# Spectral layer and squared-ReLU FFN: rows turned by DMA transposes in two chunks, preparation by numbered slots, and a drain in halves of columns

## The chip, the cores and the metric

One core of a Trainium2 chip. Times are device microseconds of a launch, medians of several runs on one chip; the profile's span is about 1.7 us shorter. Every run told of here is of the fast state. The granted TensorE clock was 0.995 to 1.000 in all of them but three, which had 0.99: two of the last experiment (e11) and one of the kernel before; they are named where they count. Everywhere else the clock plays no part.

## The reference

x has 2048 rows of 512, weights and results are bf16. B_x is not used.

```python
h  = x + irfft2(rfft2(layernorm(x)) * (w_r + 1j * w_i))
u  = layernorm(h)
h2 = h + square(relu(u @ w1 + b1)) @ w2 + b2          # w1: 512 x 1792, w2: 1792 x 512
```

## The kernel before

The transforms are matmuls in six steps. Steps 1 to 4 fill T2 (the change touches only one filler matmul there; a filler is a matmul without use, put into a gap). The rows are then taken in 16 groups of 128. For each group: `s5` (TensorE) and a copy to V and H (ScalarE), `s5b` makes R of it (VectorE), `s6` multiplies R by KI (TensorE), `s6a` adds x (VectorE), `s6b` takes statistics, `norm` makes u. u is turned (128 x 128 blocks transposed) into UT, which the FFN needs as its moving operand. TensorE writes into PSUM, from where the other engines copy. GpSimd makes hb = h + b2, which VectorE adds to the FFN's result.

The FFN goes in five chunks of 2, 3, 4, 4 and 3 groups. A chunk has 14 "up" pieces (4 matmuls each) and then its "downs" (14 matmuls a group). While one chunk is computed, the next one is prepared in between. In the traces here an engine's pieces follow in the order of the program (in e6 below a turn placed one slot later also runs after the last down), so where a piece stands in the program decides what waits for it.

```python
def transp(c, half):                      # TensorE turns, ScalarE and VectorE copy out of PSUM
    pt = bank("p7", "pp", 3, BF16)
    for d in range(2):
        for i in range(n):
            o = P * (n * d + i)
            nc.tensor.transpose(pt[:, o:o + P], us[c][:, i, bass.ts(2 * half + d, P)], ident[:])
    ...                                   # half 0: nc.scalar.copy, half 1: nc.vector.tensor_copy

def up(f):
    ph = bank("ph", "ph", 3)
    ...                                   # 4 matmuls W1 x UT -> ph
    nc.scalar.activation(rl[:, 0:n], ph[:, 0:n], ACT.Relu, bias=b1f[:, f:f + 1], scale=1.0)
    sq = nc.vector.tensor_tensor(act[:, f, 0:n], rl[:, 0:n], rl[:, 0:n], ALU.mult)
    mine = [a + f // 3] if c and f % 3 == 1 and f // 3 < b - a else ...
    for g in mine:                        # GpSimd, not before this square
        add = nc.gpsimd.tensor_tensor(hb[:, g, :], hs[:, g, :], b2b[:], ALU.add)

PLAN = {1: ((-3.33, 'ahead', 0), (-0.19, 's5b', 1), ...),  # estimated us; for chunk 1 from the start of chunk 0, for the others from the end of the chunk before
        ...}

# the drain: groups 0 and 1 alone, after the last of step 4
s5_first(0); s5_whole(1); s5b(0); s6(0); s6(1)
rest = [s5(2, True), s5(3, True)]
s6a(1); s6b(0, True); s6b(1)
...                                       # fillers, roots, norms, 8 transposes, 2 copies
for c in range(5):
    run(c)
```

## Time and profile before

| | before |
|---|---|
| time, median of 7 | 166.53 us |
| span | 164.8 us |
| first FFN matmul starts | 53.65 us |
| last FFN matmul ends | 161.49 us |
| end of the last addition on VectorE to the end of the span | 2.80 us |

Two things to read first: where TensorE, busy 93% of the span, has gaps (they can be closed), and what it does in the stretches without gaps (that can only be taken away). The prediction below shows the lines. Start of the first up of a chunk to start of the next one's is a ruler used throughout; it is 14.48, 22.01, 26.83 and 26.16 us for chunks 0 to 3.

### The profile page before, as it was taken

The page shows a single profiled execution, that of the slowest core. Times are in us where ns is not written, and L with a number is a line of the kernel's source. Part 1 is how long each engine was busy: PE and PEld are TensorE (multiplying, and loading weights), DVE is VectorE, ACT ScalarE, POOL GpSimd, SP SyncE. Part 2 cuts the span into 40 slices and gives each one's busy share as a digit, 9 for nine tenths or more (in the row PEclk, how much of TensorE's full clock was granted, in tenths as well). Part 3 has the DMA queues.
Part 4 walks back from the last instruction along what each step waited for, and adds up shares of the span by engine and source line. Part 5 has one row for each costly group of instructions (what it writes and reads, how often), then busy time and mean ns, then how long its engine had stood idle before and what let it go on. Part 6 is the DMA issues. An engine that isn't in the chain of part 4 may idle for free.

```text
span 164.8 us, 2760 instructions
## 1 busy us (share of the span) xinstructions
PE 153.8 (93%) x976; PEld 89.5 (54%) x976; DVE 126.3 (77%) x320; ACT 106.7 (65%) x201; POOL 37.9 (23%) x64
## 2 busy tenths in 40 slices
PE   3989999899998999898999999999999999999992
PEld 1356676687754874564445454444644444565471
DVE  6999899999947799589984579978479974468321
ACT  4899877999957880496932798460597654088100
POOL 7867850000100005022200223300023500044000
PEclk9999999999999999999999999999999999999999
DMA  4989399999000000100000100000200001000011
GB/s 149 359 279 91 80 187 189 389 360 149 2 0 0 4 0 2 66 4 0 0 32 32 36 0 2 0 32 32 68 2 0 0 32 36 32 32 0 0 64 32
DMA packets 12621, 11.42 MB, mean 69 GB/s; under 512 B 6976, under 2 KB 11072, under 8 KB 12608
## 3 DMA queue, kind: packets, MB, share of 16 engines
q1 hardware_dynamic: 12448, 10.33, 22.6%
q0 software_dynamic: 160, 0.92, 2.6%
q8 instruction: 7, 0.11, 0.3%
q14 instruction: 6, 0.05, 0.1%
HBM read 8.01 MB, written 2.10 MB: 61 GB/s over the span
## 4 chain that ended last, share of the span: by engine, by line
PE 68%; DVE 16%; ACT 5%; DMA 3%; POOL 2%; issue 2%; SPq 0%; ACTq 0%; DVEq 0%
PE po L827 28%; PE ph L794 25%; DMA xs<-in_A_x_dram 3%; PE p L346 2%; DVE mA L436 2%; PE po L815 2%; DVE mB L436 2%; ACT junk L209 2%; PE p L623 2%; PE p L679 2%; DVE Z L442 1%; POOL rs L224 1%; ACT rl L797 1%; DVE Z L443 1%; PE p L565 1%
## 5 line engine op out<-in xcount | busy, mean ns | idle before, releaser
L794 PE MATMUL ph<-UT,W 128*128 128x384 bf16 (+2 forms) x280 | 52.7, 336 | 1.2 <-DVE UT L881 0.6
L797 ACT ACTIVATE rl<-ph,b1f 128x384 bf16<-128x384 f32 (+2 forms) x70 | 41.7, 615 | 15.1 <-PE ph L794 13.6
L827 PE MATMUL po<-W,act 128*128 128x512 bf16 x210 | 47.3, 379 | 0.0
L801 POOL TENSOR_TENSOR hb<-hs,b2b 128x512 f32<-128x512 bf16 x16 | 18.9, 1184 | 89.2 <-DVE act L798 89.2
L794 PEld LDWEIGHTS <-W 128*128 128x128 bf16 x280 | 26.9, 98 | 21.1 <-issue 1.9
L798 DVE TENSOR_TENSOR act<-rl 128x384 bf16<-128x384 bf16 (+2 forms) x70 | 29.8, 458 | 10.1 <-ACT rl L797 10.0
L827 PEld LDWEIGHTS <-act 128*128 128x128 bf16 x210 | 20.3, 98 | 23.4
L831 DVE TENSOR_TENSOR ot<-po,hb 128x512 bf16<-128x512 f32 x15 | 10.3, 690 | 11.1 <-PE po L827 7.7
L257 PE MATMUL p<-ones 128*128 128x512 bf16 x23 | 8.2, 511 | 2.8 <-POOL ones L153 2.8
L627 DVE SCALAR_TENSOR_TENSOR hs<-p,xs 128x512 bf16<-128x512 f32 x15 | 10.0, 680 | 0.9 <-PE p L623 0.9
L683 ACT COPY UT<-p 128x768 bf16<-128x768 bf16 (+1 forms) x4 | 3.6, 906 | 10.9 <-PE p L679 10.9
L243 PE MATMUL p<-KFr,xs 128*128 128x256 bf16 x32 | 7.5, 277 | 1.2 <-DVE KFr L228 1.1
L571 ACT CAST V<-p 128x512 bf16<-128x512 f32 x14 | 8.4, 600 | 0.0
L217 DVE BATCH_NORM_STATS2 st<-xs 128x6 f32<-128x512 bf16 x12 | 7.9, 677 | 0.0
L257 PEld LDWEIGHTS <-ones 128*128 128x128 bf16 x35 | 3.9, 114 | 7.2 <-POOL ones L153 2.8
L245 PE MATMUL p<-KFr,xs 128*128 128x256 bf16 x32 | 7.3, 274 | 0.0
L638 ACT ACTIVATE junk<-hs 128x512 bf16<-128x512 bf16 x6 | 3.8, 627 | 5.5 <-DVE hs L627 5.5
L346 PE MATMUL p<-GF,Bt 128*128 128x256 bf16 x56 | 7.1, 273 | 0.0
L609 DVE TENSOR_TENSOR H<-V 128x254 bf16<-128x254 bf16 x14 | 6.9, 490 | 0.3 <-ACT V L571 0.2
L491 ACT CAST T<-p 128x1024 bf16<-128x1024 f32 x7 | 7.0, 1039 | 0.0
L623 PE MATMUL p<-R,KI 128*128 128x512 bf16 x15 | 5.7, 378 | 0.9 <-ACT rl L797 0.8
L655 ACT ACTIVATE sd<-mv,eps 128x2 f32<-128x2 f32 (+2 forms) x7 | 2.0, 295 | 6.7 <-DVE mv L642 6.6
(188 smaller groups left out, 239.2 us busy)
## 6 DMA issues: line engine op xcount, KB each, us to landing
W<-in_B_w_dram SPq DMA_DIRECT2D x2, 1792.0 KB, 10.6
out_dram<-ot SPq DMA_DIRECT2D x15, 128.0 KB, 1.8
xs<-in_A_x_dram SPq DMA_DIRECT2D x3, 512.0 KB, 6.2
WB<-in_A_w_r_dram SPq DMA_DIRECT2D x1, 578.2 KB, 6.2
WB<-in_A_w_i_dram SPq DMA_DIRECT2D x1, 578.2 KB, 7.5
xs<-in_A_x_dram SPq DMA_DIRECT2D x2, 256.0 KB, 3.6
b2b<-in_B_b_dram SPq DMA_DIRECT2D x1, 128.0 KB, 9.5
out_dram<-ot SPq DMA_DIRECT2D x2, 64.0 KB, 1.5
```

Of the source, the lines that this page charges most:

```text
L217: nc.vector.bn_stats(st[:], xs[:, g, :])
L257: nc.tensor.matmul(o, lhsT=ones[:, 0:P], rhs=ones[:], start=True, stop=True)
L346: nc.tensor.matmul(puv[:, :, e, :], lhsT=Bt[:, 2 * t + 1 - e, 2 * pr + q, :], rhs=GFv[:, t, :, e, :], start=(t == 0), stop=(t == 1))
L571: nc.scalar.copy(V[:].rearrange("p e h c -> p (e h c)"), pe[:])
L623: nc.tensor.matmul(py[:], lhsT=KI[:], rhs=Rs.pop(g)[:], start=True, stop=True)
L627: nc.vector.scalar_tensor_tensor(hs[:, g, :], Ys.pop(g)[:], WSC, xs[:, g, :], ALU.mult, ALU.add)
L794: nc.tensor.matmul(ph[:, 0:n], lhsT=W1[:, d, bass.ts(f, P)], rhs=UT[:, d, 0:n], start=(d == 0), stop=(d == ND - 1))
L797: nc.scalar.activation(rl[:, 0:n], ph[:, 0:n], ACT.Relu, bias=b1f[:, f:f + 1], scale=1.0)
L798: sq = nc.vector.tensor_tensor(act[:, f, 0:n], rl[:, 0:n], rl[:, 0:n], ALU.mult)
L801: add = nc.gpsimd.tensor_tensor(hb[:, g, :], hs[:, g, :], b2b[:], ALU.add)
L827: nc.tensor.matmul(po[:], lhsT=act[:, f, bass.ts(i, P)], rhs=W2[:, f, :], start=(f == 0), stop=(f == NF - 1))
L831: nc.vector.tensor_tensor(ot[:], po[:], hb[:, g, :], ALU.add)
```

## The change

Three things in one: (1) the rows of chunks 3 and 4 are turned by DMA transposes, one a group, instead of TensorE; (2) the preparation is placed by the number of a slot (an up, or a quarter of a group's downs) instead of by estimated time; (3) the drain of groups 0 and 1 works in halves of 256 columns and in the old PSUM pool, so that it needn't wait for that pool to be empty. The core of the diff:

```diff
+    BY_DMA = (3, 4)
+    def turn(c, i):
+        if i == 0:
+            UTs[c] = ffn.tile([P, ND, 512], BF16, tag="UT", bufs=2, name="UT")
+        if c in BY_DMA:
+            nc.sync.dma_start_transpose(out=UTs[c][:, :, P * i:P * i + P], in_=us[c][:, i, :])
+        else:
+            transp(c, i)
...
-        1: ((-3.33, 'ahead', 0),
-            (-0.19, 's5b', 1),
...
+        1: dict(s5=(-1, 1, 4), s5b=(-1, 1, 6), s6=(3, 7, 14), s6a=(3, 12, 14),
+                s6b=(9, 14, 14), rstd=(15,), norm=(16, 16, 16), turn=(20, 20)),
+        2: dict(s5=(1, 1, 3, 12), s5b=(1, 3, 11, 13), s6=(10, 10, 15, 16), s6a=(10, 10, 15, 16),
+                s6b=(13, 16, 16, 16), rstd=(17,), norm=(17, 18, 20, 18), turn=(23, 24)),
+        3: dict(s5=(4, 5, 7, 15), s5b=(4, 8, 14, 15), s6=(10, 11, 18, 18), s6a=(11, 11, 18, 18),
+                s6b=(13, 13, 20, 20), rstd=(16, 22), norm=(17, 17, 23, 23), turn=(19, 19, 23, 24)),
+        4: dict(s5=(5, 5, 5), s5b=(5, 6, 7), s6=(10, 10, 14), s6a=(10, 15, 15),
+                s6b=(14, 15, 17), rstd=(15, 22), norm=(18, 18, 22), turn=(19, 23, 22)),
...
-            for f0, f1 in ((0, 5), (5, 10), (10, NF)):
+            for f0, f1 in ((0, 4), (4, 8), (8, 11), (11, NF)):
...
-    s5_first(0)
-    s5_whole(1)
-    s5b(0)
-    s6(0)
-    s6(1)
+    halves = [mm_tile(f"p5{e}")[:, 0:256] for e in range(2)]
+    for e in range(2):
+        q5(halves[e], 0, 0, e, True, True)
+    nc.scalar.copy(od[:], halves[0])
+    for h, op in ((0, ALU.add), (1, ALU.subtract)):
+        nc.vector.tensor_tensor(R2[0][:, 256 * h:256 * h + 256], halves[1], od[:], op)
+        pe = mm_tile(f"p5w{h}")[:, 0:256]
+        for e in range(2):
+            q5(pe, 1, h, e, e == 0, e == 1)
+        nc.scalar.copy(R2[1][:, 256 * h:256 * h + 256], pe)
...
+    ps.release()
+    ps = ctx.enter_context(tc.tile_pool(name="ps2", bufs=3, space=bass.MemoryType.PSUM))
```

More of the change, by code (lines that the diff above doesn't have):

```diff
@@ L530 @@
         if pr == 8:
-            warm(mm_tile("idle")[:, 0:512], 3)
+            warm(mm_tile("idle")[:, 0:512], 2)
         if pr == 0:
@@ L538 @@
             nc.scalar.activation(junk1[:], eps[:], ACT.Sqrt, bias=eps[:])
-    ps.release()
     tab.release()
     fwd.release()
-    ps = ctx.enter_context(tc.tile_pool(name="ps2", bufs=3, space=bass.MemoryType.PSUM))
     ffn = ctx.enter_context(tc.tile_pool(name="ffn", bufs=1))
@@ L577, in s5, with s5b @@
         rest()
-    def s5_first(g):
-        two = [bank("p5o", "ph", 3), bank("p5", "pp", 3)]
-        for e in range(2):
-            for r in range(2):
-                nc.tensor.matmul(two[e][:, 0:256], lhsT=T2[:, 2 * e + r, g].rearrange("p q s -> p (q s)"),
-                                 rhs=GI[:, 2 * r + e, :], start=(r == 0), stop=(r == 1))
-        od = ffn.tile([P, 256], FP32, tag="od", bufs=4, name="od")
-        nc.scalar.copy(od[:], two[0][:, 0:256])
-        Rs[g] = two[1], od
-    def s5_whole(g):
-        pe = bank("p5", "pp", 3)
-        for h in range(2):
-            for k, lt in enumerate((1, 3, 0, 2)):
-                nc.tensor.matmul(pe[:, 256 * h:256 * h + 256], lhsT=T2[:, 2 * (lt % 2) + lt // 2, g].rearrange("p q s -> p (q s)"),
-                                 rhs=GIn[:, lt // 2, :] if h and k > 1 else GI[:, lt, :], start=(k == 0), stop=(k == 3))
-        Rs[g] = R = ffn.tile([P, 512], BF16, tag="R", bufs=3, name="R")
-        nc.scalar.copy(R[:], pe[:])
-    def s5b(g):
-        pe, od = Rs[g]
-        Rs[g] = R = ffn.tile([P, 512], BF16, tag="R", bufs=3, name="R")
-        if g == 0:
-            nc.vector.tensor_tensor(R[:, 0:256], pe[:, 0:256], od[:], ALU.add)
-            nc.vector.tensor_tensor(R[:, 256:512], pe[:, 0:256], od[:], ALU.subtract)
-            return
-        V, H = pe, od
+    def s5b(g):
+        V, H = Rs[g]
+        Rs[g] = R = ffn.tile([P, 512], BF16, tag="R", bufs=3, name="R")
         nc.vector.tensor_tensor(H[:, :, 1:128], V[:, :, 0, 1:128], V[:, :, 1, 1:128], ALU.add)
@@ L617, in s6 @@
         py = bank("p6", "pp", 3)
-        if g == 0:
-            nc.tensor.matmul(py[:], lhsT=identW[:], rhs=xs[:, 0, :], start=True, stop=False)
-            nc.tensor.matmul(py[:], lhsT=KI[:], rhs=Rs.pop(g)[:], start=False, stop=True)
-            nc.scalar.activation(hs[:, 0, :], py[:], ACT.Copy, scale=WSC, accum_out=mv2[:, 0, 0:1])
-            return
         nc.tensor.matmul(py[:], lhsT=KI[:], rhs=Rs.pop(g)[:], start=True, stop=True)
@@ L646, in on_act, with rstd, norm @@
         return g == 0 if c < 2 else (g - CHUNKS[c][0]) % 2 == 0
-    def rstd(c):
-        a, b = CHUNKS[c]
-        for par in range(2):
-            mine = [g for g in range(a, b) if on_act(c, g) != bool(par)]
+    def rstd(c, gs):
+        for act in (True, False):
+            mine = [g for g in gs if on_act(c, g) == act]
             if mine:
-                st = mine[1] - mine[0] if len(mine) > 1 else 1
-                sl = slice(mine[0], mine[-1] + 1, st)
-                nc.scalar.activation(sd2[:, sl], mv2[:, sl, 1], ACT.Sqrt, bias=eps[:], scale=1.0 if par else float(D) ** -3 if c == 0 else 1.0 / D)
-        if c == 0:
-            nc.vector.tensor_scalar(mv2[:, 0, 0:1], mv2[:, 0, 0:1], 1.0 / D, None, ALU.mult)
-        nc.vector.reciprocal(rs2[:, a:b], sd2[:, a:b])
+                sl = slice(mine[0], mine[-1] + 1, mine[1] - mine[0] if len(mine) > 1 else 1)
+                nc.scalar.activation(sd2[:, sl], mv2[:, sl, 1], ACT.Sqrt, bias=eps[:], scale=1.0 / D if act else 1.0)
+        nc.vector.reciprocal(rs2[:, gs[0]:gs[-1] + 1], sd2[:, gs[0]:gs[-1] + 1])
     CHUNKS = ((0, 2), (2, 5), (5, 9), (9, 13), (13, 16))
     us, UTs = {}, {}
-    def norm(c):
-        a, b = CHUNKS[c]
-        us[c] = u2 = ffn.tile([P, 4, D], BF16, tag="u2", bufs=2, name="u2")
-        for g in range(a, b):
-            nc.vector.tensor_scalar(u2[:, g - a, :], hs[:, g, :], mv2[:, g, 0:1], rs2[:, g:g + 1],
-                                    ALU.subtract, ALU.mult)
+    BY_DMA = (3, 4)
+    def norm(c, g):
+        if c not in us:
+            us[c] = ffn.tile([P, 4, D], BF16, tag="u2", bufs=2, name="u2")
+        nc.vector.tensor_scalar(us[c][:, g - CHUNKS[c][0], :], hs[:, g, :], mv2[:, g, 0:1], rs2[:, g:g + 1],
+                                ALU.subtract, ALU.mult)
+    def turn(c, i):
[5 more added lines that the diff above has]
+            transp(c, i)
     def transp(c, half):
@@ L672, in transp @@
         n = b - a
-        if half == 0:
-            UTs[c] = ffn.tile([P, ND, 512], BF16, tag="UT", bufs=2, name="UT")
         pt = bank("p7", "pp", 3, BF16)
@@ L688 @@
     PLAN = {
-        1: ((-3.33, 'ahead', 0),
-            (-0.19, 's5b', 1),
-            (1.74, 's5', 2),
-            (1.90, 's6', 0),
-            (2.59, 's5b', 2),
-            (3.15, 's6', 1),
-            (4.46, 's6a', 0),
-            (5.01, 's6b', 0),
-            (5.71, 's6a', 1),
-            (5.93, 's6', 2),
-            (6.26, 's6b', 1),
-            (8.49, 's6a', 2),
-            (9.04, 's6b', 2),
-            (9.66, 'rstd', 0),
-            (11.25, 'norm', 0),
-            (15.74, 't0', 0),
-            (17.95, 't1', 0),),
@@ L706 @@
-        2: ((-20.48, 's5', 0),
-            (-19.75, 's5b', 0),
-            (-19.10, 's5', 1),
-            (-18.37, 's5b', 1),
-            (-17.72, 's5', 2),
-            (-16.99, 's5b', 2),
-            (-16.34, 's5', 3),
-            (-16.27, 's6', 0),
-            (-15.71, 's6a', 0),
-            (-15.61, 's5b', 3),
-            (-14.89, 's6', 1),
-            (-14.33, 's6a', 1),
-            (-13.51, 's6', 2),
-            (-12.95, 's6a', 2),
-            (-12.13, 's6', 3),
-            (-11.94, 's6b', 0),
-            (-11.57, 's6a', 3),
-            (-10.56, 's6b', 1),
-            (-9.18, 's6b', 2),
-            (-7.80, 's6b', 3),
-            (-6.57, 'rstd', 0),
-            (-6.30, 'norm', 0),
-            (-2.74, 't0', 0),
-            (-1.51, 't1', 0),),
@@ L730 @@
-        3: ((-24.63, 's5', 0),
-            (-22.53, 's5', 1),
-            (-22.25, 's5b', 0),
-            (-20.43, 's5', 2),
-            (-20.15, 's5b', 1),
-            (-18.33, 's5', 3),
-            (-18.05, 's5b', 2),
-            (-15.99, 's6', 0),
-            (-15.95, 's5b', 3),
-            (-14.29, 's6a', 0),
-            (-13.89, 's6', 1),
-            (-13.10, 's6b', 0),
-            (-12.19, 's6a', 1),
-            (-11.79, 's6', 2),
-            (-11.00, 's6b', 1),
-            (-10.09, 's6a', 2),
-            (-9.69, 's6', 3),
-            (-8.90, 's6b', 2),
-            (-7.99, 's6a', 3),
-            (-6.80, 's6b', 3),
-            (-6.16, 'rstd', 0),
-            (-5.30, 'norm', 0),
-            (-2.35, 't0', 0),
-            (-1.48, 't1', 0),),
@@ L754 @@
-        4: ((-25.83, 's5', 0),
-            (-24.89, 's5', 1),
-            (-23.95, 's5', 2),
-            (-23.67, 's5b', 0),
-            (-22.73, 's5b', 1),
-            (-21.79, 's5b', 2),
-            (-17.57, 's6', 0),
-            (-16.63, 's6', 1),
-            (-15.69, 's6', 2),
-            (-12.12, 's6a', 0),
-            (-11.18, 's6a', 1),
-            (-10.24, 's6a', 2),
-            (-9.86, 's6b', 0),
-            (-8.92, 's6b', 1),
-            (-7.98, 's6b', 2),
-            (-6.58, 'rstd', 0),
-            (-6.48, 'norm', 0),
-            (-4.96, 't0', 0),
-            (-2.74, 't1', 0),),
-    }
@@ L775, in prep_steps @@
-    def prep_steps(c, total):
-        a, b = CHUNKS[c]
-        n = b - a
-        pieces = dict(s5=(0.22, s5), s5b=(0, s5b), s6=(0.22, s6), s6a=(0, s6a), s6b=(0, lambda g: s6b(g, on_act(c, g))),
-                      ahead=(0, lambda g: rest[1]()), rstd=(0, lambda g: rstd(c)), norm=(0, lambda g: norm(c)),
-                      t0=(0.12 * n, lambda g: transp(c, 0)), t1=(0.12 * n, lambda g: transp(c, 1)))
-        return [(t if c == 1 else total + t, pieces[p][0], lambda p=p, k=k: pieces[p][1](a + k)) for t, p, k in PLAN[c]]
+        1: dict(s5=(-1, 1, 4), s5b=(-1, 1, 6), s6=(3, 7, 14), s6a=(3, 12, 14),
+                s6b=(9, 14, 14), rstd=(15,), norm=(16, 16, 16), turn=(20, 20)),
@@ new lines, in prep_steps @@
+    def prep_steps(c):
+        a = CHUNKS[c][0]
+        n = CHUNKS[c][1] - a
+        steps = []
+        for kind, piece in (("s5", lambda k: rest[1]() if c == 1 and k == 1 else s5(a + k)), ("s5b", lambda k: s5b(a + k)),
+                            ("s6", lambda k: s6(a + k)), ("s6a", lambda k: s6a(a + k)),
+                            ("s6b", lambda k: s6b(a + k, on_act(c, a + k))),
+                            ("rstd", lambda k: rstd(c, range(a + 2 * k, min(a + 2 * k + 2, a + n)) if c in BY_DMA else range(a, a + n))),
+                            ("norm", lambda k: norm(c, a + k)), ("turn", lambda k: turn(c, k))):
+            steps += [(slot, lambda piece=piece, k=k: piece(k)) for k, slot in enumerate(PLAN[c][kind]) if slot >= 0]
+        return sorted(steps, key=lambda step: step[0])
@@ L834, in mlp_slots @@
         for f in range(NF):
-            slots.append((0.22 * (b - a), lambda f=f: up(f)))
+            slots.append(lambda f=f: up(f))
         for i in range(b - a):
-            for f0, f1 in ((0, 5), (5, 10), (10, NF)):
-                slots.append((0.22 * (f1 - f0), lambda i=i, f0=f0, f1=f1: down(i, f0, f1)))
+            for f0, f1 in ((0, 4), (4, 8), (8, 11), (11, NF)):
+                slots.append(lambda i=i, f0=f0, f1=f1: down(i, f0, f1))
         return slots
     def run(c):
-        slots = mlp_slots(c)
@@ L844, in run @@
-        prep, at = [], 0.0
-        if c + 1 < 5:
-            n = CHUNKS[c + 1][1] - CHUNKS[c + 1][0]
-            prep = prep_steps(c + 1, sum(t for t, _ in slots) + 0.68 * n)
-        for k, (t, slot) in enumerate(slots):
-            slot()
-            at += t
-            while prep and (prep[0][0] <= at or k == len(slots) - 1):
-                _, cost, piece = prep.pop(0)
-                piece()
-                at += cost
+        prep = prep_steps(c + 1) if c + 1 < 5 else []
+        for k, slot in enumerate(mlp_slots(c)):
+            slot()
+            while prep and prep[0][0] <= k:
+                prep.pop(0)[1]()
@@ L857, with q5 @@
     u2 = ffn.tile([P, 4, D], BF16, tag="u2", bufs=2, name="u2")
     UTs[0] = ffn.tile([P, ND, 512], BF16, tag="UT", bufs=2, name="UT")
-    s5_first(0)
-    s5_whole(1)
-    s5b(0)
-    s6(0)
-    s6(1)
+    def q5(o, g, h, e, first, last):
+        for r in range(2):
+            nc.tensor.matmul(o, lhsT=T2[:, 2 * e + r, g].rearrange("p q s -> p (q s)"),
+                             rhs=GIn[:, r, :] if h and e == 0 else GI[:, 2 * r + e, :], start=(first and r == 0),
+                             stop=(last and r == 1))
@@ new lines @@
+    halves = [mm_tile(f"p5{e}")[:, 0:256] for e in range(2)]
+    for e in range(2):
+        q5(halves[e], 0, 0, e, True, True)
+    R2 = [ffn.tile([P, 512], BF16, tag="R", bufs=3, name="R") for g in range(2)]
+    od = ffn.tile([P, 256], FP32, tag="od", bufs=1, name="od")
+    nc.scalar.copy(od[:], halves[0])
[5 more added lines that the diff above has]
+        nc.scalar.copy(R2[1][:, 256 * h:256 * h + 256], pe)
@@ new lines @@
+    for g in range(2):
+        py = mm_tile("p6")[:, 0:512]
+        if g == 0:
+            nc.tensor.matmul(py, lhsT=identW[:], rhs=xs[:, 0, :], start=True, stop=False)
+        for h in range(2):
+            nc.tensor.matmul(py[:, 256 * h:256 * h + 256], lhsT=KI[:], rhs=R2[g][:, 256 * h:256 * h + 256],
+                             start=(g == 1), stop=(g == 1 or h == 1))
+        if g == 0:
+            nc.scalar.activation(hs[:, 0, :], py, ACT.Copy, scale=WSC, accum_out=mv2[:, 0, 0:1])
+        else:
+            nc.vector.scalar_tensor_tensor(hs[:, 1, :], py, WSC, xs[:, 1, :], ALU.mult, ALU.add)
@@ L864 @@
+    warm(mm_tile("idle")[:, 0:512], 3)
+    ps.release()
+    ps = ctx.enter_context(tc.tile_pool(name="ps2", bufs=3, space=bass.MemoryType.PSUM))
     rest = [s5(2, True), s5(3, True)]
     idle = bank("idle", "ph", 3)
-    s6a(1)
     s6b(0, True)
-    s6b(1)
+    st1 = ffn.tile([P, 6], FP32, tag="st", bufs=4, name="st2")
+    nc.vector.bn_stats(st1[:], hs[:, 1, :])
+    warm(idle[:], 4)
+    nc.scalar.activation(sd2[:, 0:1], mv2[:, 0, 1:2], ACT.Sqrt, bias=eps[:], scale=float(D) ** -3)
     nc.vector.tensor_scalar(mv2[:, 0, 0:1], mv2[:, 0, 0:1], 1.0 / D, None, ALU.mult)
-    warm(idle[:], 9)
+    nc.vector.reciprocal(rs2[:, 0:1], sd2[:, 0:1])
@@ L871 @@
+    nc.vector.bn_aggr(mv2[:, 1, :], st1[:])
+    nc.scalar.activation(sd2[:, 1:2], mv2[:, 1, 1:2], ACT.Sqrt, bias=eps[:])
     for g in range(2):
-        nc.scalar.activation(sd2[:, g:g + 1], mv2[:, g, 1:2], ACT.Sqrt, bias=eps[:], scale=1.0 if g else float(D) ** -3)
-    for g in range(2):
-        nc.vector.reciprocal(rs2[:, g:g + 1], sd2[:, g:g + 1])
+        if g == 1:
+            nc.vector.reciprocal(rs2[:, 1:2], sd2[:, 1:2])
         nc.vector.tensor_scalar(u2[:, g, :], hs[:, g, :], mv2[:, g, 0:1], rs2[:, g:g + 1], ALU.subtract, ALU.mult)
```

## The prediction

> **What bounds the kernel now.** I read the page first, then the table of stretches, the waits of TensorE, the chain in order of time, and the timelines of the places where the chain leaves TensorE. Row 1 of the page and the list of stretches:
>
> ```profile
> PE 153.8 (93%) x976; PEld 89.5 (54%) x976; DVE 126.3 (77%) x320; ACT 106.7 (65%) x201; POOL 37.9 (23%) x64
> ...
> 45.00:53.60 8.60, 7.20 (x51) 4.10 (x51) 5.21 (x15) 5.85 (x14) 0.00 (x0) 1.00 0.00 0
> ...
> 67.00:90.00 23.00, 21.59 (x145) 12.05 (x143) 18.42 (x48) 14.67 (x34) 3.55 (x3) 1.00 0.06 18
> 90.00:117.00 27.00, 27.00 (x151) 13.17 (x150) 20.99 (x49) 16.14 (x34) 4.91 (x4) 1.00 0.06 21
> ```
>
> TensorE is the bound: after 90 us it has no gap until the end. The change touches nothing ahead of 46.2 us, nor the last stores. So there are two kinds of gain: TensorE work taken out of the FFN (53.65 to 161.5 us), and gaps closed in the drain (46.3 to 53.65) and in the first two chunks. The chain of waits names the gaps:
>
> ```profile
> 66.91 0.35 PE p L679 x6
> 67.25 0.02 issue
> 67.28 0.81 ACT UT L683
> 68.09 0.04 issue
> 68.13 0.82 PE ph L794 x4
> ```
>
> Here all downs of chunk 0 are over, then rows are turned (L679), the copy out of PSUM takes 0.81 us, and only then does chunk 1 begin. From 69 to 78.6 us the chain stays on ACT and DVE; the timelines of TensorE and DVE show why:
>
> ```profile
> 70.78 1.26 DVE L609 TENSOR_TENSOR H<-V 128x254 bf16<-128x254 bf16 x1
> ...
> 74.77 1.24 DVE L609 TENSOR_TENSOR H<-V 128x254 bf16<-128x254 bf16 x1
> ...
> 76.89 0.38 PE L623 MATMUL p<-R,KI 128*128 128x512 bf16 x1 [0.76 <-ACT rl L797]
> ```
>
> An H addition usually takes 0.28 us. These two take 1.2 us, exactly while GpSimd adds hb (70.73 and 74.66, about 1.2 us each). DVE falls behind, and L623 waits for the R that DVE makes, whatever engine the view names.
>
> **What the Trainium skill says.** (1) "TensorE: Matmul & The Clock Gate", section "Back-to-back issue gap": N/2.4 + 2.5 ns when warm. The chain agrees: 8 matmuls of 512 columns in 1.73 us (216 ns), 56 of 384 in 9.10 (162 ns), 16 transposes in 0.89 (56 ns). (2) "SBUF — State Buffer", section "Who interferes with whom": a DVE instruction with two SBUF inputs and a GpSimd one that reads SBUF exclude each other. The 1.26 us above agrees. (3) "DMA: Bandwidth & Descriptors", section "DMA Transpose (X-bar)": done on the DMA's write side, to SBUF, two-byte types; its section "Anatomy of one DMA" puts the fixed cost at some 2.0 us, mostly completion. The trace agrees roughly: the transpose of Cn (896 columns) took 1.25 us to issue and 3.0 us to land.
>
> **The change part by part.**
>
> *1. DMA transposes for chunks 3 and 4.* Removed from TensorE: 4 x 4 + 4 x 3 = 28 transposes x 0.056 = **1.57 us**; between 115 and 143 us TensorE has no gap, so all of it is on the path if the rows land in time. The four PSUM copies that go with them (ACT 1.01 and 0.80, DVE 0.69 and 0.55) were hidden.
> Do they land in time? For chunk 3, count from the start of slot 18 of chunk 2 plus its four matmuls (t = 0). s6 of the last two groups ends 0.4; s6a on DVE (0.6 each) to 1.8; statistics to about 2.7; the eviction of the second group, in order on DVE, at 2.7 to 3.3; root and reciprocal to 3.7; the two norms to 4.1 and 4.5. The queue issues the two transposes one after the other (1.25 each) at 4.2 and 5.5; landing some 2.8 later (estimate from the 3.0 of a larger one) is 8.3. TensorE reaches the next chunk after two s6 and 38 matmuls: 0.43 + 8.20 = 8.6. So hidden, with 0.3 us to spare. For chunk 4 the last two are issued about one slot earlier: 0.5 to 1 us to spare.
>
> *2. Drain.* Group 1 sets the end. Before, the copy of T by ACT ended at 46.85 but the first s5 matmul ran at 47.32, behind DVE's copy (ended 47.17) and the new pool. After: with 2 warm matmuls less one and old-pool tiles the even half starts at about 46.95, the odd half at 47.3. Group 1's first half is 4 matmuls of 256 at 47.52 to 47.96, copied by ACT (0.37) from 48.2; the second half ends 48.55 and is copied by 49.0. Before, one copy of 512 (0.59) from 48.83. So the last KI matmul goes at 49.06 instead of 49.46, is half as wide, and hs of group 1 starts at about 49.4 instead of 49.88: **0.5 us**. Group 0's hs likewise moves from 49.51 to 49.05. From there: statistics, root, and one small trap: the reciprocal of group 0 stands in DVE's order ahead of group 1's aggregate and costs about 0.1. FFN starts at 53.3 instead of 53.65: **0.35 us**. Fewer fillers (9, not 12) cost nothing: they stand in gaps.
>
> *3. Slots in chunk 0.* Turn moves ahead of the last three down matmuls (0.65 us), which cover the copies. Pure TensorE work from the first up to the next chunk's first up is 14 x 0.4375 + 0.225 + 3 x 0.216 + 28 x 0.216 + 12 x 0.056 = 13.7 us; before it took 68.13 - 53.65 = 14.48. DVE decides when the norms end: 14 squares (0.2), 2 s5b (0.95), 3 s6a (0.6), 3 statistics (0.85), root and reciprocal 0.6, norms 1.05, the first square at 1.2 us, make 12.6, against the turn at 12.4. So some 0.2 to 0.3 us is still lost: gain **0.5 us**.
>
> *4. Slots in chunk 1.* Pure work 9.10 + 9.06 + 8 x 0.22 + 0.89 = 20.8 us; before 90.14 - 68.13 = 22.0, so 1.2 us could be won. ACT has room (14 relus at 0.47 plus four V and H at 0.52 make 8.7 us in an up phase of 10.4). DVE has not. In its new order (t = 0 at the first up): squares 2 and 3 and the first two s5b as before, square 5 ends 6.6, squares 6 to 8 and the add of f = 4 to 8.6, the add of f = 7 holds square 9 until 9.7, two s6a to 11.4, third s5b to 12.6, squares 12 and 13 to 13.2, fourth s5b to 14.15. TensorE comes to the third s6 (slot 15) at 12.15 and to the fourth (slot 16) 0.87 later: it waits some 0.5, then 0.65 us. The wait moves from the up to the down phase and stays 1.1 us: gain **0.1 us**. Chunks 2 and 3 have wider ups (0.86 us a slot) and late s6: no new wait found, no gain beyond part 1.
>
> Sum: 1.57 + 0.35 + 0.5 + 0.1 = 2.5 us; 166.54 - 2.5 = **164.0 us**.
>
> **Rivals.**
> - *The wait in chunk 1 goes* (s5b done sooner than I have it, as when the GpSimd adds fall beside instructions that don't exclude them, like s6a, which ran unhindered at 79.07). For: the slots look tuned by hand, and this wait is visible. Against: DVE's work there is some 18.6 us out of 20.8, the first 1.5 idle. It would give up to 1.1 more: 162.9.
> - *The transposes land late.* For: only 0.3 us to spare; 3.0 us is from one early DMA of other size; the first one was issued in 3.2 us beside loads. Against: the queues are almost empty here (the DMA share is 0.06 to 0.08, mean 21 to 24 GB/s), and no weights load any more. A landing of 4 instead of 2.8 us costs about 0.9 for chunk 3 and perhaps 0.4 for chunk 4: 165.3.
> - *The drain gives nothing*, since the old pool must drain before the new one opens: s5 of groups 2 and 3 stand behind the hs reads and the PSUM tiles of the halves reuse buffers. "PSUM — Partial Sum Buffer", section "PSUM bank collisions raise a hardware error", asks that engines are kept apart by bank, so such tiles wait as a whole; in the trace the first s5 matmul indeed stood behind DVE's copy of another tile until 47.32. By my count there are 1.5 us for them ahead of the first turn. 164.4 if it happens.
>
> **Range and chances.** I give the middle case most of the weight, the first rival one in four, late landing one in six. This gives a range of 162.7 to 165.2. Faster by over 2% means below some 163.25 us, a gain of 3.3: that needs the first rival nearly whole with everything else as counted: 0.22. Slower by over 2% (above 169.9) would need a wait of 6 us in the place of none: 0.01. The rest is within 2%: 0.77.
>
> **What would show each step right or wrong.** Part 1: 28 transposes (L679) are gone, 7 DMA transposes of UT appear, about 1.25 us to issue and 2.5 to 3 us to land, and TensorE shows no wait for UT ahead of chunks 3 and 4. Part 2: the first up starts at 53.2 to 53.4 us, hs of group 1 at 49.4. Part 3: the gap ahead of the first up of chunk 1 is under 0.3 us, and start to start is about 14.0. Part 4: two waits of TensorE at L623 inside the downs of chunk 1, 1.1 us together, and 21.9 us start to start. The prediction would be wrong if waits for DMA stand ahead of chunks 3 and 4, if a TensorE gap over 0.5 us appears after 90 us, or if chunk 1 runs without a gap.

## The result, and the profile after

164.54 us (164.53 to 164.55) against 166.53 on the same chip, ratio 0.988 with an interval of 0.9863 to 0.9897. The gain is 2.0 us where 2.5 was predicted.

The table sets the ruler beside the terms of the predicted sum:

| stretch | before | after | gained | predicted |
|---|---|---|---|---|
| start to first up (drain) | 53.65 | 53.12 | 0.53 | 0.35 |
| chunk 0 | 14.48 | 13.77 | 0.71 | 0.5 |
| chunk 1 | 22.01 | 21.71 | 0.30 | 0.1 |
| chunk 2 (turns chunk 3) | 26.83 | 26.54 | 0.29 | 0.90 |
| chunk 3 (turns chunk 4) | 26.16 | 25.49 | 0.67 | 0.67 |
| chunk 4, to the last matmul's end | 18.36 | 18.36 | 0.0 | 0 |
| last matmul's end to the end of the span | 3.3 | 3.8 | -0.5 | 0 |

TensorE's last matmul ends 2.49 us earlier, almost the predicted sum, though two terms are off in opposite ways; then half a microsecond is lost after it. Row 1 of the page after, and the view that gives busy time by stretches, cut at the chunks (columns: us, then busy us and instructions of TensorE, its weight loads, VectorE, ScalarE, GpSimd, the granted clock, the DMA share, GB/s):

```profile
PE 152.1 (93%) x947; PEld 87.8 (54%) x947; DVE 125.4 (77%) x320; ACT 105.5 (65%) x203; POOL 36.9 (23%) x64
...
53.12:66.89 13.77, 13.77 (x104) 9.39 (x104) 12.14 (x41) 7.85 (x20) 2.27 (x2) 1.00 0.01 2
66.89:88.60 21.71, 21.16 (x135) 11.73 (x134) 18.30 (x48) 14.19 (x33) 3.55 (x3) 1.00 0.08 25
88.60:115.14 26.54, 26.20 (x133) 12.07 (x132) 20.28 (x49) 15.32 (x34) 4.73 (x4) 1.00 0.15 38
115.14:140.63 25.49, 25.49 (x128) 11.92 (x128) 17.38 (x40) 14.68 (x31) 4.61 (x4) 1.00 0.15 40
```

Chunk 0 has no gap now by this view (from starts, 0.07 us is lost ahead of chunk 1), and neither has chunk 3; chunks 1 and 2 have. The waits of TensorE after 45 us, in the kernel after (us in all, times, longest):

```profile
PE p L590 <- DVE R L586: 0.8, 2, 0.5
PE ph L693 <- DVE UT L804: 0.6, 1, 0.6
```

The first is `s6` waiting for R, now named as such. Its two places in chunk 1, and the third, in chunk 2, from the timeline of TensorE:

```profile
79.33 0.38 PE L590 MATMUL p<-R,KI 128*128 128x512 bf16 x1
...
80.81 0.38 PE L590 MATMUL p<-R,KI 128*128 128x512 bf16 x1 [0.45 <-DVE R L586]
...
106.66 0.38 PE L590 MATMUL p<-R,KI 128*128 128x512 bf16 x1 [0.34 <-DVE R L586]
```

An idle time shown there starts at the modelled end of the matmul before, so it is smaller than what is lost. Counted from starts (8 downs of 0.216 from 77.34 end their issue at 79.07) the losses are 0.26, 0.62 and 0.50 us.

For the third, VectorE's timeline shows the square that stands beside the last addition of hb in chunk 2; without an addition beside it such a square takes 0.42 us (e2, at 91.25). It ends at 102.0, and from there VectorE has no pause of over 0.15 us until the fourth R is done at 106.6:

```profile
100.77 1.23 DVE L697 TENSOR_TENSOR act<-rl 128x512 bf16<-128x512 bf16 x1 [0.28 <-ACT rl L696]
```

The DMA transposes (view of one tile, UT) take 1.2 us to issue and land 2.4 us after the start of the issue:

```profile
L639 SPq DMA_TRANSPOSE UT<-u x7: 1194/1197/1257, 107.8 to 137.3; - x7
...
DMA to landing us min/median/max: 2.4/2.4/2.5
```

Three of four rows of chunk 3 and all rows of chunk 4 land in time; the last row of chunk 3 is just late. By the packed trace it is issued at 112.60 and lands at 115.01; the first up starts at 115.14, 0.07 us after the time that the last down leaves (its start at 114.86 and 0.216). In e7 below, where this landing is on the path for certain, the first up starts the same 0.14 us after it (117.22 and 117.35).

The drain: hs of group 1 on VectorE starts at 49.24 after and at 49.88 before. First before, then after:

```profile
49.88 0.69 DVE L627 SCALAR_TENSOR_TENSOR hs<-p,xs 128x512 bf16<-128x512 f32 x1 [0.88 <-PE p L623]
50.60 0.69 DVE L641 BATCH_NORM_STATS2 st<-hs 128x6 f32<-128x512 bf16 x1
51.33 0.18 DVE L642 BATCH_NORM_AGGREGATE mv<-st 128x2 f32<-128x6 f32 x1
```

```profile
49.24 0.69 DVE L780 SCALAR_TENSOR_TENSOR hs<-p,xs 128x512 bf16<-128x512 f32 x1 [0.67 <-PE p L775]
49.96 0.69 DVE L788 BATCH_NORM_STATS2 st<-hs 128x6 f32<-128x512 bf16 x1
...
50.92 0.16 DVE L793 BATCH_NORM_AGGREGATE mv<-st 128x2 f32<-128x6 f32 x1
```

From statistics to aggregate it takes 0.96 us where it took 0.73 (50.60 to 51.33 before): part of the 0.64 is given back.

The tail. The last addition on VectorE ends at 161.95 before and 159.46 after (the ends of the chains, shown), 2.80 and 3.29 us ahead of the end of the span (164.754 and 162.755 in the packed traces; the expectations below took the spans rounded to 0.1 and so have 2.85 and 3.34).

```profile
161.53 0.42 DVE ot L817
```

```profile
159.04 0.42 DVE ot L716
```

In SP's closing sequence, a row of short waits, one each for a DMA semaphore, the trace after shows a hole in which SP runs nothing and waits for nothing. View of the closing line, before in one window and after in two narrow ones (times are first and last start):

```profile
L911 SPq EVENT_SEMAPHORE  x6: 28/28/28, 163.5 to 163.8; - x6
L911 SPq DRAIN  x2: 7/10/13, 163.9 to 164.0; - x2
```

```profile
L834 SPq EVENT_SEMAPHORE  x1: 28/28/28, 161.3 to 161.3; - x1
...
L834 SPq EVENT_SEMAPHORE  x1: 28/28/28, 161.8 to 161.8; - x1
```

Before, six of them pass in 0.3 us. After, 0.44 us lie between two neighbours. The DMA view of the last 3.5 us after (159.4 to 162.9) also has one packet on queue 14 that the kernel before has not at its end:

```profile
q14 instruction: 1, 0.01, 0.8%
```

### The profile page after: what moved, and what is told of

Read it like the earlier page. It is cut to its first block, busy times and chain, and to the rows that moved or that the text cites. A ratio compares the mean times of both kernels' runs of the same rounds, so it can differ in the third digit from the quotient of the medians.

```text
span 162.8 us, 2720 instructions
## 1 busy us (share of the span) xinstructions
PE 152.1 (93%) x947; PEld 87.8 (54%) x947; DVE 125.4 (77%) x320; ACT 105.5 (65%) x203; POOL 36.9 (23%) x64
## 4 chain that ended last, share of the span: by engine, by line
PE 66%; DVE 22%; ACT 4%; issue 3%; POOL 3%; ACTq 0%; DVEq 0%; POOLq 0%
PE po L726 26%; PE ph L693 25%; DVE act L697 3%; DVE st L217 3%; PE p L346 2%; DVE mA L436 2%; PE po L714 2%; DVE mB L436 2%; PE p L590 2%; DVE Z L442 1%; POOL rs L224 1%; DVE Z L443 1%; ACT rl L696 1%; PE p L563 1%; DVE M L452 1%
## 5 line engine op out<-in xcount | busy, mean ns | idle before, releaser
L696 ACT ACTIVATE rl<-ph,b1f 128x384 bf16<-128x384 f32 (+2 forms) x70 | 41.2, 615 | 22.5 <-PE ph L693 20.7
L693 PE MATMUL ph<-UT,W 128*128 128x384 bf16 (+2 forms) x280 | 51.6, 337 | 0.6 <-DVE UT L804 0.6
L697 DVE TENSOR_TENSOR act<-rl 128x384 bf16<-128x384 bf16 (+2 forms) x70 | 31.3, 483 | 9.3 <-ACT rl L696 9.1
L730 DVE TENSOR_TENSOR ot<-po,hb 128x512 bf16<-128x512 f32 x15 | 10.3, 688 | 12.6 <-PE po L726 11.1
L594 DVE SCALAR_TENSOR_TENSOR hs<-p,xs 128x512 bf16<-128x512 f32 x14 | 9.1, 681 | 0.0
L243 PE MATMUL p<-KFr,xs 128*128 128x256 bf16 x32 | 7.7, 283 | 0.8 <-DVE KFr L228 0.8
L245 PE MATMUL p<-KFr,xs 128*128 128x256 bf16 x32 | 7.6, 281 | 0.0
L376 ACT CAST U<-p 128x1024 bf16<-128x1024 f32 x6 | 6.2, 1059 | 0.0
L346 PEld LDWEIGHTS <-Bt 128*128 128x128 bf16 x56 | 5.4, 98 | 1.3
L620 ACT ACTIVATE sd<-mv,eps 128x1 f32<-128x1 f32 (+2 forms) x10 | 2.7, 294 | 5.1 <-DVE mv L609 5.0
L582 DVE TENSOR_TENSOR H<-V 128x254 bf16<-128x254 bf16 x14 | 6.0, 426 | 0.0
```

The lines of the kernel that those rows point to most:

```text
L243: nc.tensor.matmul(o, lhsT=xs[:, g, P * t:P * t + P], rhs=KFr[:, g, 0:P].unsqueeze(1).to_broadcast([P, 2, P]), start=True, stop=False)
L346: nc.tensor.matmul(puv[:, :, e, :], lhsT=Bt[:, 2 * t + 1 - e, 2 * pr + q, :], rhs=GFv[:, t, :, e, :], start=(t == 0), stop=(t == 1))
L594: nc.vector.scalar_tensor_tensor(hs[:, g, :], Ys.pop(g)[:], WSC, xs[:, g, :], ALU.mult, ALU.add)
L693: nc.tensor.matmul(ph[:, 0:n], lhsT=W1[:, d, bass.ts(f, P)], rhs=UT[:, d, 0:n], start=(d == 0), stop=(d == ND - 1))
L730: nc.vector.tensor_tensor(ot[:], po[:], hb[:, g, :], ALU.add)
```

## The experiments

Each is the changed kernel with one edit. All passed the comparison with the reference, and all but the ones named have the same time within 0.3% in all their runs. Of the kernel before, one run of 21 was at 168.03 us; it had the clock of 0.99. Medians are compared.

**e1: TensorE turns again.** Part 1 alone is undone.

```diff
-    BY_DMA = (3, 4)
+    BY_DMA = ()
-  3: ... rstd=(16, 22), norm=(17, 17, 23, 23), turn=(19, 19, 23, 24)
+  3: ... rstd=(22,), norm=(22, 22, 23, 23), turn=(26, 27)
-  4: ... rstd=(15, 22), norm=(18, 18, 22), turn=(19, 23, 22)
+  4: ... rstd=(22,), norm=(22, 22, 22), turn=(26, 27)
```

> The changed kernel, but the rows of chunks 3 and 4 are turned by TensorE again, in slots 26 and 27. Theory of the path: 28 transposes of 0.056 us come back, so the last matmul ends 1.5 to 1.6 us later than 159.0 us (160.5 to 160.6). Rival (the DMA transposes only moved the wait elsewhere): under 0.5 us later. On the tail: in the changed kernel the time from the end of the last ot addition on VectorE (159.46) to the end of the span is 3.34 us, before it was 2.85. If the extra 0.5 us comes from the number of instructions in the DMA queue engine's stream (7 transposes more), it goes away here and the whole kernel is only about 1.1 us slower than the changed one (165.6); if the tail is due to the new drain or the slots, it stays, and the kernel takes 166.1.

Measured: 165.56 us. The last matmul ends at 160.46, 1.47 us later than in the changed kernel (159.00); the waits for R are the same. The tail is 2.80 us (160.93 to 163.73), as short as before. So part 1 is worth 1.47 us at TensorE, but only 1.02 us of time: the transposes cost the other half microsecond at the very end. By the ruler chunk 2 takes 27.36 us here: 0.82 more than in the changed kernel (0.90 less the 0.07 of the late row), but also 0.53 more than before the change (26.83). So the wait in chunk 2 comes with the new slots, not with the DMA.

**e2: GpSimd fills instead of adding (wrong result).**

```diff
-                add = nc.gpsimd.tensor_tensor(hb[:, g, :], hs[:, g, :], b2b[:], ALU.add)
+                add = nc.gpsimd.memset(hb[:, g, :], 0.0) if c in (1, 2) else \
+                    nc.gpsimd.tensor_tensor(hb[:, g, :], hs[:, g, :], b2b[:], ALU.add)
```

> Wrong result on purpose: in chunks 1 and 2 the GpSimd additions of hb are replaced by fills that read nothing. Theory: the additions shut VectorE out when it has two SBUF inputs, so VectorE is late with R and TensorE waits at the fourth-step matmul (0.26 + 0.6 us in chunk 1, 0.25 + 0.34 in chunk 2). With fills that do not read, squares and H additions of over 1 us vanish and TensorE gains 1.0 to 1.4 us: 163.1 to 163.5. Rival (VectorE has too much work there in any case): under 0.4 us gained.

Measured: 163.07 us, 1.47 less. (The result lacks h + b2 in seven groups. The comparison still called it correct, so its tolerance does not see a term as small as this one.) The waits for R are gone. Timelines of VectorE, first in the changed kernel, then here, at the same place:

```profile
69.53 1.27 DVE L581 TENSOR_TENSOR H<-V 128x254 bf16<-128x254 bf16 x1
```

```profile
69.54 0.29 DVE L581 TENSOR_TENSOR H<-V 128x254 bf16<-128x254 bf16 x1
```

And `s6` of TensorE here, back at the times that the count of starts gives without a wait:

```profile
79.07 0.38 PE L590 MATMUL p<-R,KI 128*128 128x512 bf16 x1
...
79.94 0.38 PE L590 MATMUL p<-R,KI 128*128 128x512 bf16 x1
```

Chunk 1 takes 20.85 us (66.89 to 87.74), which is the pure TensorE work; chunk 2 takes 25.93 instead of 26.54. The fill takes half as long as the addition (0.52 against 1.16 us), so the shorter use alone could explain half of the effect; but VectorE shows no long instruction beside a fill at all. VectorE's own work does fit, and the rival falls.

**e3 and e4: one and eight useless loads more on the SP queue.**

```diff
+    for k in range(1):                                   # e4: range(8)
+        nc.sync.dma_start(spare[:, k:k + 1], B_b1[0:P].unsqueeze(1))
```

> The changed kernel with one small useless load on the SP queue after the weights. Theory of the instruction stream: SP stands still for 0.44 us in its closing sequence (161.33 to 161.77) because it fetches its next block of instructions there; a longer stream moves that point to where SP waits anyway, and the tail shrinks by 0.45 us: 164.1. Rival (the order of the eight DMA semaphores, which the seven extra transposes shifted): the tail changes too, as one DMA shifts that order. Rival (something in the drain of the DMA rings): no change, 164.5.

> The same with eight useless loads, which leave the order of the eight DMA semaphores as it is in the changed kernel. Theory of the instruction stream: the tail shrinks by 0.45 us here too (164.1), unless the point falls on another place where SP does not wait. Rival of the semaphore order: no change against the changed kernel, 164.5, while one load changes it.

Measured: 164.65 and 164.02 us. e3 is a miss: the hole is still there (161.6 to 162.0), one place earlier in the row, and the tail is 3.29 us; besides, in the profiled run (164.84 us, the slowest of the four) the first up starts 0.26 us later, which I cannot explain. So one DMA moves the point by about one instruction and not out of the sequence. e4 is a hit: the tail is 2.80 us, and six waits pass without a hole:

```profile
L837 SPq EVENT_SEMAPHORE  x6: 27/28/1193, 159.8 to 161.3; - x6
```

(1193 ns is the wait for the last store.) The packet on queue 14 now comes at 158 us, ahead of the last store, where SP waits anyway. Eight loads leave the order of the eight DMA semaphores as it is in the changed kernel, and the hole goes; one load (e3) and seven transposes fewer (e1) give one and the same order, and only e1 has no hole. So the order is not the cause. The length of SP's stream is: all 13 traces fall into two classes, a tail of 3.29 to 3.30 us and the hole with 42 or 43 DMAs on SP (the changed kernel, e2, e3, e5 to e9), 2.79 or 2.80 us and no hole with 35 or 50 (the kernel before, e1, e4, e10, e11). That the hole is the fetch of the next block of instructions is a reading of it: the packet is on queue 14 and in every kernel with the hole it comes at the end; but it comes 0.6 us after the hole, and no view says what SP does in the hole. The Trainium skill fits: "Runtime: NRT & Kernel Launch", section "Instruction fetch mechanics", says that a sequencer fetches its stream in blocks through a DMA queue of its own, and calls the cost of a block's edge "mostly hidden". If the hole is such an edge, 0.44 us of it are not hidden here; that it is one is not shown.

**e5: hb added early (right result).** The cure for what e2 showed: GpSimd adds hb of the next chunk right after that chunk's last norm, when VectorE has mostly evictions from PSUM and idle time.

```diff
-            mine = [a + f // 3] if c and f % 3 == 1 and f // 3 < b - a else range(a, b) if not c and f == NF - 1 else []
+            mine = range(a, b) if not c and f == NF - 1 else []
...                                                       # at the end of run(c):
+        for g in range(*CHUNKS[c + 1]) if c + 1 < 5 else ():
+            add = nc.gpsimd.tensor_tensor(hb[:, g, :], hs[:, g, :], b2b[:], ALU.add)
+            ...                                           # waits for the last norm of chunk c + 1
```

> Correct result. The hb additions of chunks 1 to 4 are moved on GpSimd from between the squares to right after the last norm of the chunk before, where VectorE has only evictions from PSUM (one SBUF input) and idle time. Theory of the exclusion: squares and H additions of over 1 us vanish from the ups of chunks 1 to 3, both pairs of waits at the fourth-step matmul go, TensorE ends 1.3 to 1.5 us earlier than in the changed kernel: 163.0 to 163.3. Rival (the additions then hold up the first squares of the chunk, or the copies ahead of it): up to 0.5 us of that is given back at the start of chunk 1, 163.5.

Measured: 163.06 us, the same as with the fills, and no wait of TensorE for R is left. The first squares of chunk 1 are held up once (two in 1.03 us at 68.43), which costs TensorE nothing.

**e6: chunk 1 turned after the last down.**

```diff
-  1: ... turn=(20, 20)
+  1: ... turn=(21, 21)
```

> The changed kernel with the turning of chunk 1 after the last down piece of chunk 0 instead of ahead of it, as in the kernel before. Theory of part 3: the three covering matmuls (0.65 us) no longer hide the copies out of PSUM, a wait of about 0.5 us for UT comes back ahead of chunk 1, and the kernel takes 165.0 to 165.2. Rival (the norms were late anyway, so the gap only moves): under 0.2 us.

Measured: 165.17 us, 0.63 more; the wait for UT by ScalarE (0.6 us) is back in TensorE's waits. Part 3 is that gap.

**e7: the last two norms and transposes of chunk 3 three slots later.**

```diff
-  3: ... norm=(17, 17, 23, 23), turn=(19, 19, 23, 24)
+  3: ... norm=(17, 17, 26, 26), turn=(19, 19, 26, 26)
```

> The changed kernel with the last two norms and DMA transposes of chunk 3 in slot 26 instead of 23 and 24, so behind the eviction of the third group on VectorE (ends 113.0 us). Theory: a DMA transpose takes 1.25 us to issue and 2.4 us from issue to landing, one after the other, so the last lands at about 117.1 where the first up wanted it at 115.1: a wait of TensorE of 1.8 to 2.2 us, and 166.4 to 166.7, as slow as before. Rival (the transposes overlap on the ring and land together): a wait under 1 us.

Measured: 166.73 us, no better than before the change. TensorE's waits here have a new first line:

```profile
PE ph L693 <- DMA UT<-u: 2.1, 1, 2.1
```

The transposes are issued one after the other and their landing is on the path as soon as they are late. The last one lands at 117.22 as expected, and the first up starts at 117.35.

**e9: the old drain.** The drain of the kernel before is put back, everything else stays.

> The changed kernel with the drain of the kernel before (whole rows, new PSUM pool from the start, 3 and 9 fillers). Theory: the first up starts 0.5 us later (53.6 us), nothing after it changes, and the kernel takes 165.0 to 165.1. Rival (the slots of chunk 1 depend on the drain and hide it): under 0.2 us.

Measured: 165.04 us, 0.50 more; the first up starts at 53.64.

**e8: the aggregate first.**

```diff
     nc.vector.bn_stats(st1[:], hs[:, 1, :])
+    nc.vector.bn_aggr(mv2[:, 1, :], st1[:])
...
     nc.vector.reciprocal(rs2[:, 0:1], sd2[:, 0:1])
-    nc.vector.bn_aggr(mv2[:, 1, :], st1[:])
```

> The changed kernel with one instruction moved on VectorE: the aggregate of group 1 comes right after its statistics, ahead of the reciprocal of group 0, which waits for ScalarE. Theory (the small trap named in the prediction): statistics to aggregate took 0.96 us in the changed kernel and 0.73 before, so u of group 1 and the first up come 0.1 to 0.2 us earlier: 164.35 to 164.45. Rival (the norm of group 0 sits ahead of it anyway): no change, 164.54.

Measured: 164.42 us, 0.12 less; the first up starts at 53.03 instead of 53.12.

**e10: e5, e8 and the eight loads together.**

> The early hb additions, the aggregate first and the eight useless loads together. If the three causes are independent: 163.06 - 0.45 to 0.5 for the tail - 0.1 for the drain = 162.4 to 162.6. If the position of the instruction block is not what set the tail there, 162.95.

Measured: 162.48 us (ratio to before 0.9755, interval 0.9739 to 0.9772): 2.06 us less than the changed kernel, with a right result. The gains add up within 0.06: 1.48 + 0.12 + 0.52 is 2.12. In the stretches by chunk TensorE is now busy throughout (chunk 1 shown), so what is left after the drain is its own work:

```profile
66.80:87.65 20.85, 20.85 (x136) 11.76 (x135) 16.43 (x48) 14.20 (x33) 4.97 (x5) 1.00 0.08 26
```

**e11: chunk 2 turned by DMA as well** (on top of e10, four useless loads).

```diff
-    BY_DMA = (3, 4)
+    BY_DMA = (2, 3, 4)
-  2: dict(s5=(1, 1, 3, 12), s5b=(1, 3, 11, 13), s6=(10, 10, 15, 16), s6a=(10, 10, 15, 16),
-          s6b=(13, 16, 16, 16), rstd=(17,), norm=(17, 18, 20, 18), turn=(23, 24)),
+  2: dict(s5=(1, 1, 3, 7), s5b=(1, 3, 8, 10), s6=(9, 9, 12, 13), s6a=(9, 9, 12, 13),
+          s6b=(11, 11, 14, 14), rstd=(14, 16), norm=(15, 15, 16, 16), turn=(16, 16, 17, 18)),
```

> As the last one, with the rows of chunk 2 turned by DMA too (four useless loads instead of eight, so that the SP stream is as long), and the preparation of chunk 2 two to four slots earlier, for which VectorE has room now. If the rows land in time: 16 transposes of 0.056 us less on TensorE, 161.5 to 161.8. If the norms end later than about 82.9 us, 3.9 us ahead of the first up, or ScalarE holds up the ups, a wait eats it: 162.4 or more.

Measured: 165.92 us as a median of two clusters: twice 165.09 at a clock of 1.0, twice 166.75 at 0.99. The run of the kernel before at 168.03 stands out in the same way (1.5 us longer, 0.99), so the clusters need not be this kernel's own; why the clock was lower is not shown. The profiled run is one at 165.09, and that time is compared. It is 2.6 us slower than e10. The prepared rows come too late: four issues of 1.2 us take SP from 83.2 to 88.9 us, with a store between them, and TensorE waits, first for R in the ups, then for the last row:

```profile
PE ph L696 <- DMA UT<-u: 2.2, 1, 2.2
PE p L593 <- DVE R L589: 0.9, 1, 0.9
```

The run changes the way of turning and the slots at once, so it does not show how much each of the two costs. Splitting such a chunk between both ways of turning was not tried.

## Why the prediction was right, and where it was not

- **The bound** was right: the last matmul's end moved by 2.49 us and the time followed it, apart from the tail.
- **Part 1** (1.57 us if the rows land in time): right in mechanism. e1 gives 1.47. The issue takes 1.2 us as counted, the landing 2.4 and not 2.8. But from the prediction's t = 0 (the third `s6`, at 105.94) the last row of chunk 3 is issued at 6.65 us, not at 5.5, and lands at 9.07, not at 8.3, while TensorE comes at 9.13, not at 8.6, since `s6` had held it for 0.5. So there is no 0.3 us to spare: with the 0.14 us from landing to matmul the row is 0.07 us late, which is most of what e1 lacks against 1.57. That it was so near is luck: the errors of the count (issue 1.15 later, landing 0.4 shorter, TensorE 0.5 later) nearly cancel. e7 shows that past this edge the wait is on the path.
- **Part 2** (0.35 us): the term was too small; 0.53 by the ruler, 0.50 by e9. The start of hs in group 1 moved by 0.64 instead of 0.5. The trap of the aggregate is real, and worth 0.1 (e8).
- **Part 3** (0.5 us): 0.71. I expected 0.2 to 0.3 us still lost to late norms; there is no gap. My sum of VectorE's work was wrong: its terms, as they stand, make 11.9 us, not 12.6, which is ahead of the turn at 12.4 and leaves nothing lost. e6 puts the size of the moved turn at 0.63.
- **Part 4, chunk 1** (a wait of 0.5 and one of 0.65 inside the downs): right in place and kind, 0.26 and 0.62. e2 and e5 show that GpSimd's additions make it, as the prediction supposed from 70.78 us of the profile before. So chunk 1 gained 0.30 us, not 0.1.
- **Part 4, chunk 2** ("no new wait found"): wrong. The fourth `s6` waits 0.50 us, and 0.6 us in all is lost there. The step that failed is the overlap of VectorE's preparation with the ups: the prediction gives no count for it, only wide ups and late `s6`. In the trace the square beside the last hb addition took 1.23 us, and VectorE worked from it to the fourth R without a pause that counts. It is the mechanism that the prediction had named for chunk 1 and did not apply here. e1 shows that the new slots bring it (27.36 us against 26.83 before), e2 and e5 that it goes with the additions (25.93). Of the 0.60 us, 0.50 are this wait and 0.07 the late row; they took two thirds of what chunk 3's transposes freed.
- **"The change touches nothing ... nor the last stores"**: true of the program, wrong of the time. The seven extra DMAs of the SP queue brought a stop of 0.44 us into its closing sequence. This term, not in the sum at all, is what makes the gain 2.0 instead of 2.5. e1 and e4 show that the length of the stream decides; what SP does in the stop is inferred.
- **Rivals**: the rest of the wait in chunk 1 did not go by itself (it goes with e5); the transposes were late by 0.07 us only; the drain gave its gain. By luck the errors of parts 2 and 3 and of chunk 1 (0.18, 0.21 and 0.20 too little) cancel that of chunk 2 (0.6 too much).
- **The skill's figure for TensorE**: the prediction quotes N/2.4 + 2.5 ns and leaves out that the page gives it for a single matmul, and for a stream of them less at 512 columns and more at 128 (last section). The trace, with 216 and 56 ns, decides for the formula, so the sums stand.

## What to carry to other kernels

Before work is taken off the engine that bounds the kernel, look which other engine will then be the last to finish its share: here VectorE's margin was so small that seven GpSimd additions of 1.2 us beside the wrong instructions cost TensorE 1.5 us, and moving them was worth that beside the 2.0 us of the whole change. A DMA transpose removes engine time only if the issue of the last row starts early enough (here 2.4 us to land, 1.2 of them the issue, and 0.14 more to the matmul) ahead of use, and several of them queue up, here 1.3 us apart. After a change, set the ruler also from the last useful instruction to the end of the span: instructions added to a queue may move a stop to where nothing covers it.

## What the Trainium skill lacked or had wrong

- "DMA: Bandwidth & Descriptors", section "DMA Transpose (X-bar)": the section gives no time for one transpose. Here a 128 x 512 bf16 block from SBUF to SBUF holds the issuing queue for 1.2 us (a plain store holds it 0.33) and lands 2.4 us after its issue began; four in a row need 5 us of issue (e11).
- "Runtime: NRT & Kernel Launch", section "Instruction fetch mechanics": the cost of a block's edge is "mostly hidden". In the closing sequence of a queue 0.44 us is not (tail 3.29 against 2.80 us, e4), if that stop is such an edge.
- "TensorE: Matmul & The Clock Gate", section "Back-to-back issue gap": it gives N/2.4 + 2.5 ns for a single matmul and, for a stream of weight loads and matmuls, about 131 ns at 512 columns and 81 at 128. Here streams ran at 216 ns (512 columns, 1.73 us for 8) and 56 ns (transposes of 128, 0.89 us for 16): the formula holds and the stream's figures do not.
